# Splitting the second weights of the first token group, and letting the planner choose between GpSimd and VectorE for low parts

## Chip, cores and metric

One core of one Trainium2 chip runs the whole program as a single launch. The metric is the device time of that launch in microseconds (us). Engines are named as the profile names them: PE is TensorE (PEld its weight loads), DVE is VectorE, ACT is ScalarE, POOL is GpSimd, SP is SyncE, which here issues every DMA.

## What is computed

Top-32 attention over 2 batches x 8 heads x 576 rows, then a mixture of 4 experts over the 1152 tokens, then a gated block. Cut from the reference:

```python
scores = scale * np.matmul(q, k.transpose(0, 1, 3, 2))      # 576 x 576 per head
kth = np.partition(scores, -top_k, axis=-1)[..., -top_k:-top_k + 1]
scores = np.where(scores >= kth, scores, -1000000000.0)     # then softmax, then @ v
...
for e in range(E):                                          # E = 4, D = 512, F = 1024
    h = np.maximum(x @ w1[e], 0.0)
    out += p[:, e:e + 1] * (h @ w2[e])
...
a = x @ w_a
b = x @ w_b
return (a * b @ w_out).astype(np.float32)                   # d_ff = 1536
```

Everything is float32.

## The kernel before, in words

**Tokens and groups.** The 1152 tokens are nine tiles of 128. They go through attention and experts in four groups of 1, 2, 3 and 3 tiles (numbered 0 to 3). Attention of a tile takes four steps, one for each pair of heads: scores on PE, evicted by ACT (L702); four MAX8 and three MATCH_REPLACE8 for each of two heads on DVE (L722, L730) to find the 32nd largest score; mask and softmax on ACT and POOL (L753, L757, L761, L772); transposes on PE (L460), and the product with V. After the last step of a head pair, ACT and DVE write a group's attention output as a high and a low part into `xs` (L865, L867). While attention of a later group goes on, PE fills in the expert work of an earlier one.

**Two ways to multiply.** PE multiplies full float32 operands in one long matmul, which the trace shows as two records each. Or an operand is split into a high part (rounded to `fp32r`) and the low rest, and three short fp32r matmuls, high x high, high x low and low x high, take the place of one long one. `w_unit` splits a 512 KB piece of weights: load into `raw`, ACT writes the high part into `mid` (L888), and GpSimd or VectorE subtracts to make the low part (L889). In `experts`, which serves groups 1 to 3, all operands are split. Which of the two engines makes the low part is fixed in the code by `late`: GpSimd for group 1 and for experts 0 and 1 of group 2, VectorE for the rest.

**Group 0** has one tile, and `plain` serves it without splitting. Each expert takes two halves of 512 hidden units: 16 long matmuls of 128 columns with w1 into one PSUM bank `p`, one ACT Relu into `hf` (L1063), then 4 long matmuls of 512 columns with w2, which the trace names `ps<-raw,low` and `ps<-ys,low`. That is 32 of these for the group.

**What sets the order.** All work is recorded as operations with an engine, a length, a priority and dependencies. A planner (`Plan.best`, `order`) plays them through with a list of lengths, makes 42 orders with random delays, and emits the one whose replay is shortest on average. Each engine then runs its own list strictly in order, held back by semaphores alone. An operation that is late therefore holds everything behind it on its engine, and a change of one operation can move any other.

Of the kernel before, what the change touches and what calls it, by code (L numbers as in the profile page):

```python
# [79 lines left out]


class Op:
    __slots__ = ("engine", "hold", "lag", "key", "emit", "waits", "after", "tiles", "n", "start", "left", "at", "nbytes", "port", "since", "late")

# [11 lines left out]
class Plan:  # L96
# [3 lines left out]
    def add(self, engine, hold, emit, key, after=(), tiles=(), lag=100, nbytes=0, port=False):  # L100
        op = Op()
        op.engine, op.hold, op.lag, op.key, op.emit = engine, hold, lag, key, emit
        op.waits = list({id(a): a for a in after if a is not None}.values())
        op.tiles = list({id(t): t for t in tiles}.values())
        op.after, op.n, op.start, op.nbytes, op.port, op.since = [], len(self.ops), None, nbytes, port, 0.0
        op.late = 0.0
        self.ops.append(op)
        return op

    def best(self):  # L110

        found = None
        for r in range(ORDERS):
            draw = random.Random(r)

            since = STAGES[r * len(STAGES) // ORDERS]
            for op in self.ops:
                if r:  # L120
                    op.late = found[3][op.n] if found[4][op.n] < since else draw.uniform(0.0, SHAKE)
            got = self.order()
            mean = sum(self.rerun(got, random.Random(i)) for i in range(RERUNS)) / RERUNS
            if LOG:
                print("order", r, since, self.span, mean)
            if found is None or mean < found[0]:
                found = mean, got, {id(t): t.slot for op in got for t in op.tiles}, [op.late for op in self.ops], [op.start for op in self.ops]
        for op in found[1]:
            for t in op.tiles:
                t.slot = found[2][id(t)]  # L130
        return found[1]
# [30 lines left out]
    def order(self):  # L162
# [7 lines left out]
                t.users += 1  # L170
        for op in self.ops:
            op.left, op.at = len(op.waits), op.since
            for w in op.waits:
                w.after.append(op)
        late, ready, free, events, tick = {}, {}, {}, [], 0
# [42 lines left out]
        def pick(engine):  # L218
            late_, ready_ = late[engine], ready[engine]
            while late_ and late_[0][0] <= now:  # L220
                _, _, op = heapq.heappop(late_)
                heapq.heappush(ready_, (op.key, op.n, op))
            skipped, found = [], None
            stuck = set()
            while ready_:
                item = heapq.heappop(ready_)
                op = item[2]

                ok = not (op.port and free.get("POOL", 0.0) > now)
# [12 lines left out]
            return found  # L242

        while len(done) < len(self.ops):
            moved = False
            for engine in free:
# [8 lines left out]
                for t in op.tiles:  # L255
                    if t.slot is None:
                        t.slot = place(t)
                        t.slots.free.discard(t.slot)
                        t.slots.next += 1
                op.start = now  # L260
                done.append(op)
                if engine == "SP":
                    free[engine] = now + ISSUE
# [13 lines left out]
            while queue and queue[0][0] <= now:  # L277
# [10 lines left out]
                for a in op.after:  # L288
                    a.left -= 1
                    a.at = max(a.at, now + (SEEN_PE if a.engine == "PE" else SEEN))  # L290
                    if not a.left:
                        heapq.heappush(late[a.engine], (a.at, a.n, a))
# [10 lines left out]
def dve(n):  # L303
    return 62 + 1.04 * n


def pool_(n):
    return 105 + 2.2 * n
# [11 lines left out]
LATE = 2  # L320

FILL = 9
SLACK = 1200

URGENT = 3


def body(tc, q, k, v, probs, w1, w2, wa, wb, wo, out):
# [553 lines left out]
    def w_unit(src, a, late):  # L882
# [4 lines left out]
        ld = load(lambda: r.ap.rearrange("p (a n) -> p a n", a=a), lambda: src, 500 + s, (), [r], 512 << 10)  # L887
        hi = scalar(1024, lambda: nc.scalar.activation(u.ap[:, 0:1024], r.ap, AF.Copy), 500 + s, [ld], [u, r], sbuf=True)  # L888
        sub = lambda eng: eng.tensor_tensor(u.ap[:, 1024:2048], r.ap, u.ap[:, 0:1024], op=ALU.subtract)  # L889
        if late:  # L890
            lo = vector(dve(1024), lambda: sub(nc.vector), 500 + s if late > 1 else -100, [hi], [u, r], port=True)
        else:
            lo = gpsimd(pool_(1024), lambda: sub(nc.gpsimd), -100, [hi], [u, r])
        return u, [hi, lo], lambda i: u.ap[:, i * 1024:(i + 1) * 1024].rearrange("p (a n) -> p a n", a=a)

    plains = [0]
# [41 lines left out]
    def experts(c):  # L938
# [7 lines left out]
        yd, sums_ = {}, {}  # L946
        for e in range(E):

            late = 2 if c == len(GROUPS) - 1 else c == len(GROUPS) - 2 and e >= LATE
            for f0 in range(0, F, 512):  # L950
                hts, units = [], []
                for u in range(f0, f0 + 512, 256):
# [73 lines left out]
    def plain(c):  # L1026
# [5 lines left out]
        for e in range(E):  # L1032
            last2 = None
            for f0 in range(0, F, 512):
                p = ms.tile()
                p2 = p2 if f0 else ms.tile()
                h = hfs.tile()
                last = None
                us = []
                for u in range(0, 512, 256):  # L1040
# [11 lines left out]
                if e == 0 and f0 == 0:  # L1052

                    for a in range(KD):
# [5 lines left out]
                                )  # L1060

                        last = tensor(4 * mm_f(128), emit, 1000 + nxt(), [last] + us[0][1] + us[1][1] + xdone[c, a], [p, us[0][0], us[1][0]])
                hd = scalar(512, lambda h=h, p=p: nc.scalar.activation(h.ap, p.ap, AF.Relu), -1000, [last], [h, p])  # L1063
                for u in range(0, 512, 256):
                    r, rd, rv = plain_unit(w2[e, f0 + u:f0 + u + 256].rearrange("(a p) n -> p a n", p=128), 2)
# [166 lines left out]
```

## Time and profile before

| | |
|---|---|
| median of 3 runs | 841.64 us (841.16 to 842.02) |
| profiled execution, its device time | 841.12 us |
| its span, first to last instruction | 839.3 us |
| PE, DVE, ACT, POOL busy | 817.1, 707.0, 536.5, 266.0 us |
| mean granted TensorE clock | 0.997 |

The span is the profiled execution alone, and 1.8 us of its device time lie outside it. "Busy" is the union of an engine's instruction records. Records of one engine overlap a little, so the time that an instruction takes from its successor is read from start to start, not from its length.

### The profile page before, as it was taken

The numbers are of one execution on the slowest core, as the hardware profiler recorded it, in microseconds if no ns is written. First come the engines' busy times: TensorE is split into PE (matmuls) and PEld (weight loads), VectorE is DVE, ScalarE is ACT, GpSimd is POOL, SyncE is SP. The second block draws the span as 40 slices with busy tenths as digits, with TensorE's granted clock in tenths as the row PEclk, the third lists the DMA queues.
The fourth block names the chain that finished last, engine by engine and source line by source line (L and its number), as shares of the span: only waits on it lengthen the run. The fifth ranks groups of instructions, "written<-read, shape, count | busy, mean of one in ns | idle before, by whom it ended". The sixth has DMA issues, their size and how long they took to land.

```text
span 839.3 us, 14126 instructions
## 1 busy us (share of the span) xinstructions
PE 817.1 (97%) x5177; PEld 729.6 (87%) x5177; DVE 707.0 (84%) x1371; ACT 536.5 (64%) x1029; POOL 266.0 (32%) x250
## 2 busy tenths in 40 slices
PE   7599999999999999999999999999999999999997
PEld 6477787789888889889889998998898989999996
DVE  7999999999999999999969999545235889899723
ACT  6888887989989898887666555343125535344220
POOL 3634443897997966654110000000000000000000
PEclk9999999999999999999999999999999999999999
DMA  5849977755554445323345656443002322323003
GB/s 174 288 123 310 311 237 240 227 164 179 180 178 150 155 147 182 102 76 101 101 126 163 213 158 220 126 125 101 1 1 60 91 78 74 101 77 100 26 1 112
DMA packets 83509, 117.06 MB, mean 139 GB/s; under 512 B 10608, under 2 KB 54640, under 8 KB 83440
## 3 DMA queue, kind: packets, MB, share of 16 engines
q1 hardware_dynamic: 83440, 116.17, 44.0%
q8 instruction: 40, 0.66, 0.3%
q14 instruction: 29, 0.24, 0.1%
HBM read 109.07 MB, written 7.08 MB: 138 GB/s over the span
## 4 chain that ended last, share of the span: by engine, by line
PE 80%; DVE 16%; ACT 3%; issue 1%; POOL 0%; DVEq 0%; POOLq 0%; ACTq 0%
PE ps L457 75%; DVE low L722 8%; DVE low L730 7%; PE ps L460 4%; ACT low L772 1%; ACT mid L888 0%; POOL mid L889 0%; ACT low L827 0%; ACT low L702 0%; ACT low L753 0%; DVE low L793 0%; ACT low L761 0%; DVE low L1171 0%; DVE ys L1079 0%; DVE xs L867 0%
## 5 line engine op out<-in xcount | busy, mean ns | idle before, releaser
L722 DVE MAX8 low<-low 128x8 f32<-128x576 f32 x288 | 203.9, 747 | 1.7 <-ACT low L702 1.7
L457 PE MATMUL ps<-xs,mid 128*128 128x384 f32 (+1 forms) x1152 | 203.9, 321 | 0.0
L457 PE MATMUL ps<-mid 128*128 128x512 f32 x768 | 197.5, 395 | 0.4 <-POOL mid L889 0.4
L457 PEld LDWEIGHTS ps<-xs,mid 128*128 128x128 f32 x1152 | 185.1, 189 | 9.2 <-issue 1.9
L457 PEld LDWEIGHTS ps<-mid 128*128 128x128 f32 x768 | 139.6, 188 | 23.7 <-POOL mid L889 1.0
L730 DVE MATCH_REPLACE8 low<-low 128x576 f32<-128x576 f32 x216 | 159.4, 744 | 0.0
L457 PE MATMUL ps<-xs,big 128*128 128x384 f32 x864 | 152.6, 335 | 0.0
L457 PEld LDWEIGHTS ps<-xs,big 128*128 128x128 f32 x864 | 150.2, 188 | 1.5 <-DVE xs L1020 0.3
L888 ACT ACTIVATE mid<-raw 128x1024 fp32r<-128x1024 f32 x96 | 101.7, 1059 | 42.0 <-PE ps L457 31.8
L889 POOL TENSOR_TENSOR mid<-raw,mid 128x1024 fp32r<-128x1024 f32 x48 | 115.3, 2408 | 12.9 <-ACT mid L888 8.8
L757 POOL TENSOR_TENSOR low<-low 128x576 f32<-128x576 f32 x70 | 99.5, 1438 | 24.7 <-ACT low L753 24.3
L889 DVE TENSOR_TENSOR mid<-raw,mid 128x1024 fp32r<-128x1024 f32 x48 | 59.4, 1237 | 23.5 <-ACT mid L888 23.0
L958 ACT ACTIVATE mid<-ps 128x384 fp32r<-128x384 f32 (+1 forms) x96 | 43.4, 454 | 52.2 <-PE ps L457 51.5
L457 PE MATMUL ps<-big,mid 128*128 128x512 f32 x324 | 76.1, 391 | 0.0
L457 PEld LDWEIGHTS ps<-big,mid 128*128 128x128 f32 x324 | 60.5, 188 | 12.6 <-DVE low L1171 0.6
L962 DVE SCALAR_TENSOR_TENSOR mid<-ps,mid 128x384 fp32r<-128x384 f32 (+1 forms) x96 | 48.0, 506 | 23.0 <-ACT mid L958 22.8
L1150 ACT ACTIVATE low<-ps 128x384 f32<-128x384 f32 x36 | 17.7, 492 | 70.1 <-PE ps L457 70.0
L772 ACT ACTIVATE low<-low 128x576 f32<-128x576 f32 x70 | 51.1, 773 | 13.1 <-DVE low L769 13.1
L753 ACT ACTIVATE low<-low 128x576 f32<-128x576 f32 x70 | 52.2, 776 | 6.7 <-POOL low L747 6.7
L761 ACT ACTIVATE low<-low 128x576 f32<-128x576 f32 x70 | 54.3, 778 | 2.1 <-POOL low L757 1.8
L460 PE MATMUL ps<-identr,low 128*128 128x128 f32 (+1 forms) x360 | 51.1, 284 | 4.4 <-ACT low L772 3.8
L702 ACT ACTIVATE low<-ps 128x576 f32<-128x576 f32 x72 | 46.4, 649 | 11.9 <-POOL low L757 6.6
(90 smaller groups left out, 1025.9 us busy)
## 6 DMA issues: line engine op xcount, KB each, us to landing
raw<-in_moe_w_dram SPq DMA_DIRECT2D x122, 512.0 KB, 3.7
big<-kscr SPq DMA_DIRECT2D x20, 576.0 KB, 5.1
low<-in_v_dram SPq DMA_DIRECT2D x24, 256.0 KB, 3.6
low<-in_moe_w_a_dram SPq DMA_DIRECT2D x12, 512.0 KB, 4.2
low<-in_moe_w_b_dram SPq DMA_DIRECT2D x12, 512.0 KB, 3.8
low<-in_moe_w_out_dram SPq DMA_DIRECT2D x12, 512.0 KB, 3.6
kscr<-big SPq DMA_DIRECT2D x8, 576.0 KB, 4.7
ys<-in_moe_w_dram SPq DMA_DIRECT2D x6, 512.0 KB, 4.9
```

The costliest lines, as they stand in the source:

```text
L457: nc.tensor.matmul(out, l, r, **kw)
L460: nc.tensor.transpose(out, a, i)
L702: S, lambda: nc.scalar.activation(s.ap.rearrange("p (c n) -> p c n", c=2), at.ap[:, :, 0:HALF], AF.Copy),
L722: 62 + 1.04 * width, lambda at=at, cs=cs: nc.vector.max(m8v()[:, x, cs], at()), key + 0.02 * r, [done],
L730: lambda at=at, cs=cs: nc.vector.match_replace(out=src[1](), in_to_replace=m8v()[:, x, cs], in_values=at(), imm_value=LOW),
L753: S, lambda x=x, s=s: nc.scalar.activation(e[x].ap, s.ap, AF.Relu, bias=endv()[:, x, 1:2], scale=-STEEP),
L757: pool_(S), lambda x=x, s=s: nc.gpsimd.tensor_tensor(e[x].ap, s.ap, e[x].ap, op=ALU.subtract), ks, [a], [s, e[x]]
L761: lambda x=x: nc.scalar.activation(e[x].ap, e[x].ap, AF.Exp, bias=endv()[:, x, 0:1], scale=scale, accum_out=sums.ap[:, x:x + 1]),
L772: S, lambda x=x: nc.scalar.activation(e[x].ap, e[x].ap, AF.Copy, scale=sums.ap[:, x:x + 1]),
L888: hi = scalar(1024, lambda: nc.scalar.activation(u.ap[:, 0:1024], r.ap, AF.Copy), 500 + s, [ld], [u, r], sbuf=True)
L889: sub = lambda eng: eng.tensor_tensor(u.ap[:, 1024:2048], r.ap, u.ap[:, 0:1024], op=ALU.subtract)
L962: lambda h=h, p=p: nc.vector.scalar_tensor_tensor(h.ap[:, n:2 * n], p.ap[:, 0:n], 0.0, h.ap[:, 0:n], op0=ALU.max, op1=ALU.subtract),
```

## The change

`plain` takes the second weights of experts 1 to 3 of group 0 through `w_unit`. Relu now gives two tiles in `mid`: the high part by ACT and the low part by DVE, a SCALAR_TENSOR_TENSOR from PSUM. Each long matmul with w2 becomes three short ones. Expert 0 of the group keeps its eight long ones. Low parts made by `w_unit` get a second engine: the planner takes DVE where it is free first and POOL otherwise. Only experts 1 to 3 of group 3 keep DVE as a fixed choice. The core of the diff:

```diff
+                if op.start is not None:
+                    continue
+
+                ok = not ((op.port or engine != op.own[0]) and free.get("POOL", 0.0) > now)
...
+                if engine != op.own[0]:
+                    op.engine, op.hold, op.lag, op.key = op.other
+                    op.port = True
...
+                        for w in [a.engine] + ([a.other[0]] if a.other else []):
+                            heapq.heappush(late[w], (a.at, a.n, a))
...
+APART = (1, 2, 3)
...
-        if late:
-            lo = vector(dve(1024), lambda: sub(nc.vector), 500 + s if late > 1 else -100, [hi], [u, r], port=True)
+        if late > 2:
+            lo = vector(dve(1024), lambda: sub(nc.vector), 500 + s, [hi], [u, r], port=True)
         else:
-            lo = gpsimd(pool_(1024), lambda: sub(nc.gpsimd), -100, [hi], [u, r])
+            lo = gpsimd(pool_(1024), lambda: sub(nc.vector if lo.engine == "DVE" else nc.gpsimd), -100, [hi], [u, r])
+            if True:
+
+                lo.other = "DVE", dve(1024), 90, 490
...
-            late = 2 if c == len(GROUPS) - 1 else c == len(GROUPS) - 2 and e >= LATE
+            late = (2 if e == 0 else 3) if c == len(GROUPS) - 1 else c == len(GROUPS) - 2 and e >= LATE
...
+                if e in APART:
+
+                    hi, lo = hs_.tile(), hs_.tile()
+                    hd = [scalar(512, lambda h=hi, p=p: nc.scalar.activation(h.ap[:, 0:512], p.ap, AF.Relu), -1000, [last], [hi, p])]
+                    hd.append(vector(
+                        dve(512),
+                        lambda h=hi, l=lo, p=p: nc.vector.scalar_tensor_tensor(
+                            l.ap[:, 0:512], p.ap, 0.0, h.ap[:, 0:512], op0=ALU.max, op1=ALU.subtract
+                        ),
+                        -1000, hd, [hi, lo, p],
+                    ))
+                    for u in range(0, 512, 256):
+                        r, rd, rv = w_unit(w2[e, f0 + u:f0 + u + 256].rearrange("(a p) n -> p a n", p=128), 2, False)
+                        for i in range(2):
...
+                                for m, (a, w) in enumerate(((hi, 0), (hi, 1), (lo, 0))):
+                                    mm(p2.ap, a.ap[:, cs], rv(w)[:, i], start=(f == 0 and m == 0), stop=(f + 128 == F and m == 2))
+
+                            last2 = tensor(3 * mm_r(512), emit, 1000 + nxt(), [last2] + hd + rd, [p2, r, hi, lo])
+                    continue
```

Counted over the whole built program, the instructions that differ in number are these: PE 24 long matmuls of 512 columns fewer and 72 short ones more; ACT 12 high parts of weights more (its six Relu only change their target); DVE 6 low parts of hidden units more and 24 low parts of weights fewer (24 in place of 48); POOL 36 low parts of weights more (84 in place of 48). The number and size of the loads stay as they are, but the two w2 loads that went to `ys` now go to `raw`.

The change also moves other work, since the planner makes a new order. On DVE, the place is the end of group 0's experts, where DVE hands the attention output of group 1 to PE. First the list before (`xs<-ps,xs 128x256` is the low part of group 1's last head pair, MAX and MATCH_REPLACE are the top-k of group 2):

```order
L730 MATCH_REPLACE low<-low 128x576 x2
L722 MAX low<-low 128x8 x4
L730 MATCH_REPLACE low<-low 128x576 x2
L722 MAX low<-low 128x8
L867 TENSOR_TENSOR xs<-ps,xs 128x256
L722 MAX low<-low 128x8
```

And the list of the changed kernel at that place (`mid<-ps,mid 128x512` is the last of the six low parts of hidden units, `ys<-ps,pr,ys` adds an expert's output):

```order
L734 MAX low<-low 128x8 x4
L781 RECIPROCAL low<-low 128x2
L742 MATCH_REPLACE low<-low 128x576
L1083 SCALAR_TENSOR_TENSOR mid<-ps,mid 128x512
L742 MATCH_REPLACE low<-low 128x576
L734 MAX low<-low 128x8 x2
L742 MATCH_REPLACE low<-low 128x576 x2
L734 MAX low<-low 128x8 x2
L742 MATCH_REPLACE low<-low 128x576 x2
L734 MAX low<-low 128x8
L781 RECIPROCAL low<-low 128x2
L734 MAX low<-low 128x8
L1117 SCALAR_TENSOR_TENSOR ys<-ps,pr,ys 128x512
L879 TENSOR_TENSOR xs<-ps,xs 128x256
```

The `xs` part stands behind 107 MAX in the first list and behind 112 in the second, and six low parts of hidden units have come in ahead of it.

On PE, the same place: the last matmuls of group 0 (w2 of expert 3) and the first of group 1's experts (`xs,mid`). Before (`ps<-raw,low 128x512` is a long matmul with w2, `identr,low` are transposes of probabilities):

```order
L457 MATMUL ps<-xf,ys 128x128 x4
L460 MATMUL ps<-identr,big 128x128 x6
L457 MATMUL ps<-raw,low 128x512 x2
L457 MATMUL ps<-xs,mid 128x256 x3
L457 MATMUL ps<-raw,low 128x512
L457 MATMUL ps<-xs,mid 128x256 x3
L457 MATMUL ps<-raw,low 128x512
L457 MATMUL ps<-xs,mid 128x256 x6
L460 MATMUL ps<-identr,low 128x128 x4
```

In the changed kernel (`ps<-mid 128x512 x3` is one long matmul with w2 as three short ones):

```order
L469 MATMUL ps<-xf,ys 128x128 x8
L469 MATMUL ps<-mid 128x512 x3
L472 MATMUL ps<-identr,low 128x128 x4
L472 MATMUL ps<-identr,low 64x128
L472 MATMUL ps<-identr,low 128x128 x4
L472 MATMUL ps<-identr,low 64x128
L469 MATMUL ps<-mid 128x512 x3
L469 MATMUL ps<-xs,mid 128x256 x3
L469 MATMUL ps<-mid 128x512 x3
L469 MATMUL ps<-big 128x288 x4
L469 MATMUL ps<-low 64x128 x8
L469 MATMUL ps<-low,vrem_72 64x128 x2
```

The first matmuls with w2 now stand directly behind the w1 matmuls (`xf,ys`) whose Relu they need, and a whole step of attention (`identr,low` to `low,vrem`) stands between them and the rest of the first expert matmuls.

On POOL, low parts of weights now begin in the middle of group 1's attention (`low<-low 128x576` is the subtraction of the mask, `mid<-raw,mid` a low part of weights); before, the next 20 rows of the list have none:

```order
L769 TENSOR_TENSOR low<-low 128x576 x2
L901 TENSOR_TENSOR mid<-raw,mid 128x1024
L778 TENSOR_SCALAR low<-low 128x2
L901 TENSOR_TENSOR mid<-raw,mid 128x1024
L759 TENSOR_TENSOR low<-low,facs 128x4
L769 TENSOR_TENSOR low<-low 128x576 x2
L901 TENSOR_TENSOR mid<-raw,mid 128x1024
L778 TENSOR_SCALAR low<-low 128x2
```

All the 12 new low parts, and all the others that had the choice, stand in POOL's list.

## Rows read from the trace of the kernel before

**Rows 1.** The page: span, busy time of each engine, chain that ended last.

```profile
span 839.3 us, 14126 instructions
...
PE 817.1 (97%) x5177; PEld 729.6 (87%) x5177; DVE 707.0 (84%) x1371; ACT 536.5 (64%) x1029; POOL 266.0 (32%) x250
...
PE 80%; DVE 16%; ACT 3%; issue 1%; POOL 0%; DVEq 0%; POOLq 0%; ACTq 0%
```

**Rows 2.** Busy time by stretch: stretch, length, busy us and instructions of each engine.

```profile
60.00:160.00 100.00, 98.95 (x740) 77.59 (x741) 100.00 (x215) 85.78 (x175) 48.93 (x54) 1.00 0.85 269
160.00:440.00 280.00, 279.48 (x2092) 250.22 (x2092) 270.61 (x559) 240.66 (x481) 192.09 (x153) 1.00 0.45 144
```

**Rows 3.** Timeline of PE: start, us, instruction; pace of long and short w2 matmuls.

```profile
62.23 1.02 PE L457 MATMUL ps<-raw,low 128*128 128x512 f32 x2
63.09 1.05 PE L457 MATMUL ps<-xf,ys 128*128 128x128 f32 x8
...
451.81 4.72 PE L457 MATMUL ps<-mid 128*128 128x512 f32 x20
456.37 0.69 PE L457 MATMUL ps<-xs,mid 128*128 128x384 f32 x3
```

**Rows 4.** Groups of instructions: count | busy us, mean ns | idle before them.

```profile
L889 POOL TENSOR_TENSOR mid<-raw,mid 128x1024 fp32r<-128x1024 f32 x48 | 115.3, 2408 | 12.9 <-ACT mid L888 8.8 <-DVE low L722 2.0 <-DVE low L730 0.7
L888 ACT ACTIVATE mid<-raw 128x1024 fp32r<-128x1024 f32 x96 | 101.7, 1059 | 42.0 <-PE ps L457 31.8 <-issue 9.6 <-ACT low L1116 0.4
L889 DVE TENSOR_TENSOR mid<-raw,mid 128x1024 fp32r<-128x1024 f32 x48 | 59.4, 1237 | 23.5 <-ACT mid L888 23.0 <-PE ps L457 0.4
```

**Rows 5.** Timeline of DVE around the hand-over to group 1.

```profile
143.62 0.07 DVE L730 MATCH_VALUE_LOAD low<-low 128x8 f32 x1
...
144.34 0.08 DVE L730 MATCH_VALUE_LOAD low<-low 128x8 f32 x1
...
145.73 0.41 DVE L867 TENSOR_TENSOR xs<-ps,xs 128x256 fp32r<-128x256 f32 x1
146.05 0.75 DVE L722 MAX8 low<-low 128x8 f32<-128x576 f32 x1
...
154.37 0.75 DVE L1079 SCALAR_TENSOR_TENSOR ys<-ps,pr,ys 128x512 f32<-128x512 f32 x1
155.03 0.09 DVE L730 MATCH_VALUE_LOAD low<-low 128x8 f32 x1
```

**Rows 6.** Timeline of PE at the same place.

```profile
143.71 1.09 PE L457 MATMUL ps<-low 128*64 128x128 f32 x16
...
144.95 0.80 PE L457 MATMUL ps<-big 128*128 128x288 f32 x4
145.59 1.05 PE L457 MATMUL ps<-xf,ys 128*128 128x128 f32 x8
146.39 0.71 PE L460 MATMUL ps<-identr,big 128*128 128x128 f32 x6
146.94 1.13 PE L457 MATMUL ps<-xf,ys 128*128 128x128 f32 x8
...
153.94 1.43 PE L460 MATMUL ps<-identr,low 128*128 128x128 f32 x10
155.13 0.95 PE L457 MATMUL ps<-xs,mid 128*128 128x256 f32 x6
...
158.85 3.76 PE L457 MATMUL ps<-xs,mid 128*128 128x256 f32 x30
162.45 2.62 PE L457 MATMUL ps<-mid 128*128 128x512 f32 x10
```

**Rows 7.** Busy time from the first new split to the end of attention for group 1.

```profile
77.00:140.00 63.00, 62.85 (x479) 49.45 (x478) 63.00 (x138) 53.63 (x112) 26.08 (x32) 1.00 0.86 282
```

**Rows 8.** Waits of PE from 160 to 440 us: releaser: us, times, longest.

```profile
PE ps L457 <- POOL mid L889: 0.4, 1, 0.4
```

**Rows 9.** The stretch in which the granted clock falls (third last column).

```profile
39.00:47.00 8.00, 6.27 (x45) 5.24 (x46) 8.00 (x18) 7.81 (x19) 4.84 (x8) 0.79 0.10 18
```

More of the change, by code (lines that the diff above doesn't have):

```diff
@@ L82 @@
 class Op:
-    __slots__ = ("engine", "hold", "lag", "key", "emit", "waits", "after", "tiles", "n", "start", "left", "at", "nbytes", "port", "since", "late")
+    __slots__ = ("engine", "hold", "lag", "key", "emit", "waits", "after", "tiles", "n", "start", "left", "at", "nbytes", "port", "late", "since", "other", "own")
 SEEN, SEEN_PE = 45, 130
@@ L106, in add @@
         op.late = 0.0
+        op.other, op.own = None, (engine, hold, lag, key, port)
         self.ops.append(op)
@@ L126, in best @@
             if found is None or mean < found[0]:
-                found = mean, got, {id(t): t.slot for op in got for t in op.tiles}, [op.late for op in self.ops], [op.start for op in self.ops]
+                found = mean, got, {id(t): t.slot for op in got for t in op.tiles}, [op.late for op in self.ops], [op.start for op in self.ops], [op.engine for op in self.ops]
         for op in found[1]:
+            op.engine = found[5][op.n]
             for t in op.tiles:
@@ L172, in order @@
             op.left, op.at = len(op.waits), op.since
+            op.engine, op.hold, op.lag, op.key, op.port = op.own
             for w in op.waits:
@@ L221, in pick @@
                 _, _, op = heapq.heappop(late_)
-                heapq.heappush(ready_, (op.key, op.n, op))
+                heapq.heappush(ready_, (op.key if engine == op.own[0] else op.other[3], op.n, op))
             skipped, found = [], None
@@ L227, in pick @@
                 op = item[2]
-                ok = not (op.port and free.get("POOL", 0.0) > now)
+                if op.start is not None:
+                    continue
+                ok = not ((op.port or engine != op.own[0]) and free.get("POOL", 0.0) > now)
                 for t in op.tiles:
@@ L291, in order @@
                     if not a.left:
-                        heapq.heappush(late[a.engine], (a.at, a.n, a))
+                        for w in [a.engine] + ([a.other[0]] if a.other else []):
+                            heapq.heappush(late[w], (a.at, a.n, a))
                         heapq.heappush(queue, (a.at, -1, None))
@@ L1036, in plain @@
                 p2 = p2 if f0 else ms.tile()
-                h = hfs.tile()
                 last = None
@@ L1062, in plain, with emit @@
                         last = tensor(4 * mm_f(128), emit, 1000 + nxt(), [last] + us[0][1] + us[1][1] + xdone[c, a], [p, us[0][0], us[1][0]])
+                if e in APART:
[11 more added lines that the diff above has]
+                        for i in range(2):
+                            f = f0 + u + i * 128
+                            def emit(f=f, s=u // 128 + i, i=i, rv=rv, hi=hi, lo=lo, p2=p2):
+                                cs = slice(s * 128, (s + 1) * 128)
+                                for m, (a, w) in enumerate(((hi, 0), (hi, 1), (lo, 0))):
+                                    mm(p2.ap, a.ap[:, cs], rv(w)[:, i], start=(f == 0 and m == 0), stop=(f + 128 == F and m == 2))
+                            last2 = tensor(3 * mm_r(512), emit, 1000 + nxt(), [last2] + hd + rd, [p2, r, hi, lo])
+                    continue
+                h = hfs.tile()
                 hd = scalar(512, lambda h=h, p=p: nc.scalar.activation(h.ap, p.ap, AF.Relu), -1000, [last], [h, p])
```

## The prediction

> **What bounds the kernel now.** I read the page first. PE is busy for 817.1 of 839.3 us, and the chain of work that ended last runs over PE for 80% and over DVE for 16% [rows 1]. This looks like a kernel in which whatever is taken off PE comes off the time. The next view is busy time by stretch, because the change acts in one stretch: the first long w2 matmul of those shown runs at 62 us [rows 3], and group 0's experts end where group 1's begin, near 155 us. From 60 to 160 us PE is busy for 98.95 of 100 us, but DVE is busy for 100.00 of 100 us [rows 2]. The reader is to see that two engines are full at once. Work taken off one of them is worth nothing where the other's list holds it back. ACT has 14 us free there and POOL 51. From 160 to 440 us PE is busy for 279.48 of 280 us [rows 2], and its waits there add up to 0.4 us [rows 8]. So from the first experts of group 1 on, PE alone sets the end: the end moves by as much as that start moves, plus what PE gains or loses behind it.
>
> So the question is when PE gets to group 1's experts. I take one place that both lists have, and behind which both hold the same work: the second of six matmuls `xs,mid` that stand behind the w2 matmuls of group 0. In the list as built it is the first that waits for DVE's `xs` part of the last head pair. Behind it the changed list holds the same PE instructions as before, but for five transposes of probabilities more and four transposes of `ys` fewer (0.1 us). Before, PE runs it at 155.25 us: the six begin at 155.13, and one takes 0.12, from 30 in the 3.60 us between 158.85 and 162.45 [rows 6].
>
> **The change part by part.**
>
> *PE, less work.* A long w2 matmul takes 0.86 us from its start to the next one's (62.23 to 63.09), a short one 0.228 us (20 of them from 451.81 to 456.37) [rows 3]. 24 x 0.86 = 20.6 us go and 72 x 0.228 = 16.4 us come: 4.2 us less. By PE's work alone the place would be reached at 155.25 - 4.2 = 151.0 us.
>
> *DVE, more work in the full stretch.* Each half of an expert now needs a low part of 512 hidden units, a SCALAR_TENSOR_TENSOR from PSUM, which the trace does not show in this size. The nearest rows are the accumulation of 512 columns from PSUM, 0.66 us to the next start (154.37 to 155.03), and twice a subtraction of 256 columns from PSUM, 2 x 0.32 = 0.64 us (145.73 to 146.05) [rows 5]. I take 0.65, so six make 3.9 us. A gain is excluded: nothing leaves DVE's list ahead of this place. I counted both lists. Up to the sixth of these low parts, the changed list holds exactly what the list of before holds up to its 79th MATCH_REPLACE (106 MAX and all else equal), plus the six. That MATCH_REPLACE begins at 143.62 and gives way to the next at 144.34 [rows 5]. DVE has no pause there [rows 2], so the sixth low part cannot end before 144.34 + 3.9 = 148.2 us.
>
> *PE, held by it.* The third short matmul of expert 3's second half multiplies this low part. PE's list then holds, up to the place: 10 short w2 matmuls (2.3 us), 13 expert matmuls (13 x 0.12 = 1.6), 15 transposes of probabilities (10 in 155.13 - 153.94 = 1.19, so 1.8), 12 of queries (six in 146.94 - 146.39 = 0.55, so 1.1), two lots of four score matmuls (145.59 - 144.95 = 0.64 each, 1.3), one product with V (144.95 - 143.71 = 1.24) and 4 transposes of `ys` (0.5, as those of probabilities) [rows 6]. That is 9.8 us, so the place comes at 158.0 us, 2.7 us later than before. The saved 4.2 us are all used up, and about 7 us (158.0 - 151.0) of new waiting shows on PE ahead of the place. The bounds: some of these prices hold a switch between kinds of matmuls, and at 0.5 us less in all the shift is 2.2 us; below that it cannot go as long as DVE's rows cost what they did.
>
> *ACT, more work.* Twelve high parts at 1.06 us [rows 4] are 12.7 us. From 77 to 140 us ACT was busy for 53.63 of 63 us [rows 7]; over the 71 us from 77 to 148 that rate makes 60.4 us. With the twelve it is 73.1 us, 2.1 us more than there is. Records overlap a little, so the true excess lies between nothing and 2.1 us. ACT feeds both the low parts and the top-k, so what it lacks delays DVE. I take 0.7 us, nearer to nothing, since the changed list still lets DVE go on with top-k meanwhile.
>
> *POOL.* Twelve low parts at 2.41 us [rows 4] are 28.9 us in a stretch with 51 us free; hidden. Without that cover each would hold a mask subtraction for up to 2.4 us, and a softmax behind it. The 24 low parts that go from DVE to POOL are 24 x 1.24 = 29.8 us less on DVE [rows 4], but all in groups 2 and 3, where PE hardly waits: 0.4 us at most to gain [rows 8]. POOL has 88 us free from 160 to 440 us [rows 2] and nothing to do after. The w2 loads are as many as before; two go to another buffer. Nothing is queued behind them that PE waited for in the trace.
>
> *Sum.* 2.7 + 0.1 + 0.7 = 3.5 us. The profiled execution took 841.12 us, so 844.6; the median of the runs is 841.64, 0.52 more, so I predict 845.1 us.
>
> **A price from the clock.** PE's new idle time, 7 us in pieces over some 75 us, has a risk of its own. From 39 to 47 us, where PE was busy for only 6.27 of 8 us, the granted clock averaged 0.79 [rows 9], so part of it ran at 1.2 GHz and the rest at 2.4: 8 x 0.21 = 1.7 us of PE work were lost. The Trainium skill, in TensorE: Matmul & The Clock Gate, section HAM oscillation, warns that idle gaps send the clock back to half rate and that each such fall costs its warm-up again. By this rule the change pays for its gaps, which is the third rival below; by the full-clock rows alone it pays nothing.
>
> **The rivals.**
>
> *The saved matmul time comes off the end.* 841.64 - 4.2 = 837.4 us. For it speak PE's share of the chain and its 98.95 of 100 us. It needs DVE not to hold PE, so the six low parts to end by 141 us, 7 us before DVE's list can give the last one. I see no row that shortens that list. Chance 0.10, mostly for an error in my counting.
>
> *Nearly nothing changes.* The shift at the hand-over is 2.2 us, ACT's excess is nothing, and PE wins back its 0.4 us of waiting and a little of the switching between the two kinds of matmuls, which falls away for the 24: 841.64 + 2.2 - 0.4 - 0.5 = 842.9, and less if more falls away. Chance 0.20.
>
> *The clock falls.* If it falls once in the last 10 us ahead of the place or behind it, 1.7 us come on top: 846.8 us; twice, 848.5. A fall earlier than 148 us costs nothing, because PE waits for DVE there anyway. It is decided by whether PE's new gaps lie together or apart. Against it: PE still has some 90% to do. Chance 0.12.
>
> *The likeliest*, a hand-over delayed by DVE's list with PE at full clock: 843.4 to 847.0 us, around 845.1. Chance 0.58.
>
> **How the numbers follow.** About 0.2% (1.7 us) is what a measurement of this kernel tells from no change, so "same" is 840.0 to 843.3 us. Faster is the first rival, 0.10. Same is the second, 0.20. Slower is the third and the likeliest, 0.70. The range leaves out the first rival and the far end of the third, where the clock falls twice: 840.5 to 848.5 us.
>
> **What would show it.** In the profile after: PE busy for some 92 of 100 us from 60 to 160 us, DVE still at 100. PE's largest new waits in that stretch end with the low parts of hidden units (L1083) or with the Relu ahead of them (L1080). The last L1083 ends at 148 us or later. The `xs` part L879 of the last head pair follows it, and the second of six `xs,mid` matmuls comes near 158 us. ACT is at 95% or more from 77 to 148 us. POOL's 12 low parts are at 2.4 us each, and DVE is idle for longer from 400 us on, without a change of the end. The prediction is wrong if the last L1083 ends before 144 us; if L1083 takes much less than 0.6 us; or if PE, once in group 1, makes up time that the trace of before does not show as waiting.

## The result, and the profile after

The changed kernel takes 847.38 us (median of four runs, 847.23 to 847.61) against 841.4 us for the kernel before (four runs, 841.12 to 842.02): a ratio of 1.0071, 95% interval 1.0058 to 1.0083. It is slower, as predicted, and inside the range, but by 6.0 us and not by 3.5, and above the 847.0 us up to which the likeliest case went. Its profiled execution took 847.46 us, 6.34 more than the one of before.

The first view is the page after: span, busy time, and the chain that ended last.

```profile
span 845.7 us, 14212 instructions
...
PE 814.0 (96%) x5201; PEld 735.2 (87%) x5201; DVE 700.4 (83%) x1353; ACT 546.7 (65%) x1041; POOL 353.0 (42%) x286
...
PE 81%; DVE 7%; ACT 6%; POOL 2%; DMA 2%; issue 2%; POOLq 0%; ACTq 0%
```

Against [rows 1], PE is busy for 3.1 us less and the span is 6.4 us longer. DVE's share of the chain fell from 16% to 7%; ACT, POOL and a DMA came in. Next, busy time by stretch (start and end, length, then PE, PEld, DVE, ACT, POOL, granted clock, DMA share, GB/s):

```profile
0.00:60.00 60.00, 42.51 (x268) 36.21 (x270) 51.85 (x117) 44.30 (x96) 24.78 (x43) 0.72 0.58 176
60.00:160.00 100.00, 92.03 (x729) 77.97 (x726) 99.97 (x214) 91.07 (x176) 73.41 (x62) 1.00 0.82 266
160.00:440.00 280.00, 279.38 (x2102) 252.73 (x2103) 264.71 (x563) 246.72 (x495) 217.90 (x168) 1.00 0.45 144
39.00:47.00 8.00, 4.96 (x23) 4.21 (x23) 8.00 (x18) 5.71 (x13) 4.64 (x7) 0.60 0.23 50
47.00:51.00 4.00, 4.00 (x28) 3.39 (x28) 3.26 (x10) 3.05 (x8) 1.68 (x3) 0.51 0.01 3
```

From 60 to 160 us PE is busy for 92.03 of 100 us, where [rows 2] had 98.95; DVE is as full as before. Behind 160 us PE works as it did. In the start the clock stands lower than in [rows 9], and down to 51 us: 0.51 from 47 to 51 us, where before it was back at 1.00. (The 0.72 of the first row can't be set against the kernel before: its trace records no clock ahead of 34.8 us, where its matmuls ran at the half pace too, from 15 to 25 us the 288-column ones at 0.24 us each, against 0.135 at full clock.) Now PE's waits in the stretch ahead of group 1 (us, times, longest):

```profile
PE ps L472 <- ACT low L784: 3.7, 3, 2.3
PE ps L472 <- ACT low L714: 1.1, 1, 1.1
PE ps L469 <- DVE mid L1083: 0.9, 1, 0.9
PE ps L469 <- DMA raw<-in_moe_w_dram: 0.9, 1, 0.9
PE ps L469 <- ACT mid L1080: 0.7, 1, 0.7
PE ps L469 <- ACT low L1101: 0.5, 1, 0.5
```

They add up to 7.8 us from 60 to 165 us. The largest are not the ones that the prediction looked for, L1083 or L1080 (0.9 and 0.7 us), but L784, the scaled softmax weights. And 0.9 us went to a load, where the prediction saw none that PE would wait for. And DVE's waits from 0 to 60 us:

```profile
DVE low L781 <- POOL low L778: 2.3, 3, 1.3
DVE big L527 <- ACT big L525: 2.0, 2, 1.8
DVE identr L493 <- POOL xf masks.py:199: 1.3, 1, 1.3
DVE low L805 <- ACT low L799: 1.2, 1, 1.2
DVE low L734 <- ACT low L714: 0.9, 1, 0.9
```

The same view of before has none at the RECIPROCAL, which is L781 here and was L769:

```profile
DVE big L515 <- ACT big L513: 1.8, 2, 1.7
DVE low L722 <- ACT low L702: 1.4, 1, 1.4
DVE identr L481 <- POOL xf masks.py:199: 1.3, 1, 1.3
```

That is 4.5 us before and 7.7 after. The timeline shows the rows (start, duration, what; in brackets the idle time before it):

```profile
27.14 0.17 DVE L781 RECIPROCAL low<-low 128x2 f32<-128x2 f32 x1 [0.54 <-POOL low L778]
36.85 0.17 DVE L781 RECIPROCAL low<-low 128x2 f32<-128x2 f32 x1 [1.28 <-POOL low L778]
47.85 0.17 DVE L781 RECIPROCAL low<-low 128x2 f32<-128x2 f32 x1 [0.47 <-POOL low L778]
52.02 0.82 DVE L805 SCALAR_TENSOR_TENSOR low<-low 128x576 f32<-128x576 f32 x1 [1.19 <-ACT low L799]
...
112.82 2.38 POOL L901 TENSOR_TENSOR mid<-raw,mid 128x1024 fp32r<-128x1024 f32 x1 [1.14 <-ACT mid L900]
113.41 0.75 DVE L1117 SCALAR_TENSOR_TENSOR ys<-ps,pr,ys 128x512 f32<-128x512 f32 x1
115.09 0.59 ACT L1080 ACTIVATE mid<-ps 128x512 fp32r<-128x512 f32 x1
115.28 0.21 POOL L778 TENSOR_SCALAR low<-low 128x2 f32<-128x2 f32 x1
115.53 0.16 DVE L781 RECIPROCAL low<-low 128x2 f32<-128x2 f32 x1
115.73 1.44 ACT L784 ACTIVATE low<-low 128x576 f32<-128x576 f32 x2
116.56 0.76 PE L472 MATMUL ps<-identr,low 128*128 128x128 f32 x5 [2.29 <-ACT low L784]
...
151.04 0.68 DVE L1083 SCALAR_TENSOR_TENSOR mid<-ps,mid 128x512 fp32r<-128x512 f32 x1
161.43 0.96 PE L469 MATMUL ps<-xs,mid 128*128 128x256 f32 x6
```

Above, DVE's new pauses: 0.54 + 1.28 + 0.47 + 1.19 = 3.5 us. In the new order these rows stand ahead of MAX rows that they used to follow, and DVE stands still for the softmax chain (exp on ACT, sum on POOL). Below, the place of the prediction: the second of the six `xs,mid` of the last row runs at 161.6 us by its own record. Before, the six began at 155.13 [rows 6], here at 161.43: 6.3 us later, the whole of what the execution lost. The middle rows are taken up below.

To compare kernels of different content I count PE's work: each matmul at the median distance from its shape's start to the next start behind 60 us, over all runs. "Done" is that sum at 60 us; "left" is the rest at 180 us, when group 0's experts are over. The last column is the profiled execution against before's 841.12; the runs are from several chips, on which the medians of the kernel before differ by up to 0.7 us.

```
kernel               done at 60   left at 180   against before   execution
before                  27.8         638.6             -              -
after                   25.6         645.1           +6.5           +6.3
after, e8               27.1         642.0           +3.4           +3.4
before, e9              26.1         640.5           +2.0           +2.0
after, e10              25.3         640.9           +2.3           +5.4
before, e11             24.6         644.4           +5.9           +5.2
```

By this count the change took 4.1 us of work off PE (776.4 to 772.3), as predicted. At 60 us PE is 2.2 us behind; from 60 to 180 us it does 101.6 in place of 110.0 us, of which 4.1 no longer exist and 4.3 were lost. So two losses are to be explained: 2.2 us in the start, and in the stretch behind it 4.3 us on top of the whole saving.

### The profile page after: what moved, and what is told of

It is laid out like the page before. It is cut to its first block, busy times and chain, and to the rows that moved or that the text cites. A ratio compares the mean times of both kernels' runs of the same rounds, so it can differ in the third digit from the quotient of the medians.

```text
span 845.7 us, 14212 instructions
## 1 busy us (share of the span) xinstructions
PE 814.0 (96%) x5201; PEld 735.2 (87%) x5201; DVE 700.4 (83%) x1353; ACT 546.7 (65%) x1041; POOL 353.0 (42%) x286
## 4 chain that ended last, share of the span: by engine, by line
PE 81%; DVE 7%; ACT 6%; POOL 2%; DMA 2%; issue 2%; POOLq 0%; ACTq 0%
PE ps L469 75%; PE ps L472 6%; DVE low L734 2%; DVE low L742 2%; POOL big L529 1%; DMA low<-in_q_dram 1%; ACT low L784 1%; ACT low L773 1%; POOL low L769 1%; ACT low L765 1%; ACT low L839 1%; ACT low L714 1%; POOL mid L901 0%; ACT mid L900 0%; DMA low<-in_moe_w_a_dram 0%
## 5 line engine op out<-in xcount | busy, mean ns | idle before, releaser
L901 POOL TENSOR_TENSOR mid<-raw,mid 128x1024 fp32r<-128x1024 f32 x84 | 204.2, 2434 | 47.0 <-ACT mid L900 41.5
L469 PE MATMUL ps<-mid 128*128 128x512 f32 x840 | 219.1, 396 | 2.5 <-DVE mid L1083 0.9
L469 PEld LDWEIGHTS ps<-mid 128*128 128x128 f32 x840 | 151.3, 188 | 28.4 <-DVE mid L1083 1.7
L900 ACT ACTIVATE mid<-raw 128x1024 fp32r<-128x1024 f32 x108 | 114.0, 1058 | 35.3 <-PE ps L469 32.4
L769 POOL TENSOR_TENSOR low<-low 128x576 f32<-128x576 f32 x70 | 99.0, 1432 | 23.5 <-ACT low L765 22.5
L714 ACT ACTIVATE low<-ps 128x576 f32<-128x576 f32 x72 | 46.7, 650 | 13.3 <-POOL low L769 10.5
L784 ACT ACTIVATE low<-low 128x576 f32<-128x576 f32 x70 | 51.5, 780 | 5.7 <-DVE low L781 5.7
L469 PE MATMUL ps<-big 128*128 128x288 f32 x256 | 52.3, 332 | 0.8 <-ACT low L714 0.8
```

What stands on the lines that cost most here:

```text
L469: nc.tensor.matmul(out, l, r, **kw)
L714: S, lambda: nc.scalar.activation(s.ap.rearrange("p (c n) -> p c n", c=2), at.ap[:, :, 0:HALF], AF.Copy),
L769: pool_(S), lambda x=x, s=s: nc.gpsimd.tensor_tensor(e[x].ap, s.ap, e[x].ap, op=ALU.subtract), ks, [a], [s, e[x]]
L784: S, lambda x=x: nc.scalar.activation(e[x].ap, e[x].ap, AF.Copy, scale=sums.ap[:, x:x + 1]),
```

## The experiments

Each run is compared with the kernel before on the same chip. In the expectations, "group 1's experts" and "group 1's second to fourth expert" mean the first group's, which the text above calls group 0. The function `later` of some runs moves rows of VectorE's list by so many places and merges the lists again so that all dependencies hold; the lists of the other engines stay as they were.

**e1: the RECIPROCALs later.**

```diff
+    moves = list(zip(early, (1, 2, 1))) + [(hurry[1], 1), (hurry[0], 1)]
...
-    for op in plan.best():
+    for op in later(plan.best()):
```

> The changed kernel with one edit: in VectorE's list the RECIPROCALs of the first three steps stand one, two and one rows later, and the first L805 stands behind one MAX of the next step; every other list is the same. My theory: VectorE's list sets when group 1's last head pair ends, and the changed kernel's list pauses 0.54, 1.28, 0.47 and 1.19 us at these four rows, 3.5 us in all, which the list before did not. Without the pauses the place moves 3.5 us ahead and the time goes from 847.4 to 843.9 us, 845 if half of the first scores come late then. Rival one, only the six added SCALAR_TENSOR_TENSORs and the weights' splits cost: 847.4, no change, since VectorE would wait elsewhere. Rival two, the clock that falls to half around 41 to 51 us costs it: 847.4 with the same fall of the clock.

848.45 us, ratio 1.0076 (1.0063 to 1.0088): no gain. The pauses at these four rows went from 3.5 to 0.2 us, but others of DVE grew, so that its waits up to 60 us fell by 2.1 us (7.7 to 5.6), and PE runs its row of 151.77 us at 150.43, 1.3 us earlier and not 3.5:

```profile
DVE low L781 <- POOL low L778: 0.2, 1, 0.2
150.43 0.50 PE L469 MATMUL ps<-mid 128*128 128x512 f32 x1 [1.03 <-DVE mid L1083]
```

Then the clock takes that back (windows, columns as above):

```profile
148.00:151.00 3.00, 1.30 (x6) 0.83 (x7) 3.00 (x8) 2.44 (x4) 2.83 (x4) 1.00 0.64 208
151.00:155.00 4.00, 4.00 (x18) 3.44 (x17) 4.00 (x9) 4.00 (x10) 4.00 (x4) 0.57 0.69 230
```

Behind a stretch with 1.30 of 3 us busy, PE ran at a mean of 0.57 for 4 us: 1.7 us of work lost. The profiled execution is the fastest of the five (847.21 us); whether the clock fell in the others too isn't known. So this run doesn't decide on the pauses, but it doesn't bear out their full price either.

**e2: the added VectorE rows short.**

```diff
-l.ap[:, 0:512], p.ap, 0.0, h.ap[:, 0:512], op0=ALU.max, op1=ALU.subtract
+l.ap[:, 0:16], p.ap[:, 0:16], 0.0, h.ap[:, 0:16], op0=ALU.max, op1=ALU.subtract
```

> The changed kernel with the same lists, but the six SCALAR_TENSOR_TENSORs (L1083) work on 16 of 512 columns, and the third matmul takes the high part of the hidden values in place of the low part, so that the low part of the hidden values is left out. My theory: VectorE's list holds the end of the stage, so six rows of about 0.1 us in place of 0.69 us give back 6 x 0.57 = 3.4 us: 844.0 us. Rival, TensorE or ScalarE holds it: 847.4 us, no change.

847.7 us, 1.0067 (1.0054 to 1.0081): nothing, as the rival said. The six rows took 163 ns each in place of 683, and yet PE's longest wait for L784 stands at the same place, no earlier and no shorter than the 2.29 us at 116.56 above:

```profile
117.28 0.76 PE L472 MATMUL ps<-identr,low 128*128 128x128 f32 x5 [2.36 <-ACT low L784]
```

This is where my theory fell: VectorE's six added rows are not, by themselves, what the end waits for.

**e3: both edits.** Diffs as in e1 and e2.

> Both edits: the later RECIPROCALs and the six short SCALAR_TENSOR_TENSORs, lists else the same; the low part of the hidden values is left out. My theory: the two add up, 3.5 + 3.4 = 6.9 us, which is less than the 7.8 us that TensorE waits between 60 and 165 us in the changed kernel: 840.5 us, near the kernel before without being much under it, since TensorE's saving of 4.2 us would then begin to show; 842 if ScalarE (66.1 of 71 us busy between 77 and 148 us) holds TensorE before that. Rival, TensorE's clock or order sets the time: over 845 us.

846.93 us, 1.006 (1.0048 to 1.0073), far from 840.5. The rival, over 845, holds for the number. Its clock fell at 151 us as in e1.

**e4: the free choice of engine alone.**

```diff
-APART = (1, 2, 3)
+APART = ()
```

> The changed kernel with no expert's second weights taken apart: only the choice between GpSimd and VectorE for the low parts, and the order that follows from it, are left of the change. VectorE's rows of the first stage come out the same as in the changed kernel, with the RECIPROCALs of the first steps ahead of the rows that they followed before. My theory: its place is late by the pauses of the start alone, 3.5 us, and has no added SCALAR_TENSOR_TENSORs: about 841.4 + 3.5 = 844.9 us. Rival, the pauses cost nothing and only taking the weights apart does: 841.4 us.

845.96 us, 1.0051 (1.0039 to 1.0064), nearer to the theory than to the rival. PE's work was 2.1 us behind at 60 us and no more than 2.0 at 180. The rest, some 2.8 us, was lost later, most of it in a fall of the clock:

```profile
460.00:468.00 8.00, 6.17 (x27) 5.84 (x26) 5.93 (x8) 3.43 (x6) 3.73 (x2) 0.79 0.68 197
```

So the theory came near in the number by some luck: the start cost 2 us and not 3.5. What the run does show is the stretch from 60 to 180 us: with DVE's pauses in the start, but without the weights taken apart, PE did 110.2 us of work there, as before (110.0), and is busy for 98.71 of the 100 us from 60 to 160. In the changed kernel that stretch holds the larger loss. It comes in with the taking apart, or with the order that the planner then makes.

**e5, e6: the taking apart of the weights short, on POOL alone and on POOL and ACT.**

```diff
-sub = lambda eng: eng.tensor_tensor(u.ap[:, 1024:2048], r.ap, u.ap[:, 0:1024], op=ALU.subtract)
+sub = lambda eng: eng.tensor_tensor(u.ap[:, 1024:1024 + m], r.ap[:, 0:m], u.ap[:, 0:m], op=ALU.subtract)
...
-r, rd, rv = w_unit(w2[...], 2, False)
+r, rd, rv = w_unit(w2[...], 2, False, 16)
... in e6 also
-hi = scalar(1024, lambda: nc.scalar.activation(u.ap[:, 0:1024], r.ap, AF.Copy), ...
+hi = scalar(1024, lambda: nc.scalar.activation(u.ap[:, 0:m], r.ap[:, 0:m], AF.Copy), ...
```

> The changed kernel with the same lists; of the second weights of group 1's second to fourth expert GpSimd takes only 16 of 1024 columns of each unit's low part (L901, 12 units), and the matmul with the low weights takes the high ones, so that these low parts are left out. The first theory has fallen with the shortened SCALAR_TENSOR_TENSORs, which gave nothing; the new one is that the taking apart of the weights stands inside the softmax chain in the in-order lists: TensorE waits 3.7 us for the scaled weights (L784), ahead of which stand L901 on GpSimd (2.4 us each, ahead of L778) and L900 on ScalarE (1.05 us each). If GpSimd's part is what holds the chain, the time falls by most of 3.7 us, to about 844 us. Rival, ScalarE's part holds it: it falls by the one wait that L901 sets alone, about 0.9 us at 116 us, to 846.5 us. Rival two, neither: 847.4 us.

> As the run before, and ScalarE too takes only 16 of 1024 columns of these 12 units (L900); the matmuls take the hidden values as their right side, so the second weights are left out. Lists as in the changed kernel. New theory (the taking apart stands in the softmax chain on ScalarE and GpSimd): the waits of TensorE for L784 (3.7 us), for L714 (1.1) and for L1080 (0.7) go for the most part, so 4 to 5 us: 842.5 to 843.5 us, and the VectorE row L1083 shows 0.9 us of wait or is covered. Rival, the order of the lists and the start hold the time: 847.4 us.

e5: 846.99 us, 1.0067 (1.0053 to 1.0081), the second rival or, within the interval, the first. The theory, 844, missed. e6: 849.21 us, 1.009 (1.0072 to 1.0108), with runs from 847.24 to 852.37: with less to do on ACT and POOL the kernel was not faster, and its median was slower. The theory, 843.5 at most, missed, and the rival's 847.4 is at the lower end of the runs. Its profiled execution, the slowest of them, shows why that one was: three falls of the clock, each worth 6 x 0.28 = 1.7 us:

```profile
104.00:110.00 6.00, 5.05 (x26) 4.72 (x27) 6.00 (x13) 3.12 (x7) 3.75 (x5) 0.72 0.95 327
118.00:124.00 6.00, 4.96 (x24) 4.08 (x26) 6.00 (x13) 4.33 (x10) 1.62 (x2) 0.72 0.77 261
155.00:161.00 6.00, 5.31 (x24) 4.64 (x24) 6.00 (x14) 5.21 (x12) 5.92 (x5) 0.72 0.30 98
```

**e7, e8: with the later RECIPROCALs, and then with the short VectorE rows too.** Diffs as in e1, e2 and e6.

> As the run before, with the RECIPROCALs of the first three steps and the first L805 later in VectorE's list. Alone, that made the stage up to 150 us 1.4 us shorter, and a fall of the granted clock to half at 151 us, behind the waits of 148 to 151 us, took it back. Without those waits the clock should stand, and the 1.4 us should show: 841 to 842 us. Rival, the start costs nothing at the end: the time of the run before.

> As the run before, and the six SCALAR_TENSOR_TENSORs (L1083) on 16 of 512 columns: nearly all that the change adds to ScalarE, GpSimd and VectorE is gone (second weights and the low part of the hidden values are left out), and TensorE's shorter list is left. If added work on the three engines and the start are the whole loss, TensorE's 4.2 us come out: 841.4 - 4.2 + 0.9 (what the start still lags by at 60 us) = 838.1 us. Rival, VectorE's list still holds the stage (it is 0.9 us later than before by the start, and has no added work): 841 to 842 us, and TensorE waits for it.

e7: 847.46 us, 1.0072 (1.005 to 1.0095). The theory missed. The six runs fall into three from 845.1 to 845.8 and three from 849.1 to 851.3 us, so the median is a time that none of them took, and whether the rival, e6's time, holds can't be told. The profiled one, of the faster three, has a fall of the clock at 150 us again. e8: 845.95 us, 1.0045 (1.0033 to 1.0057), where the theory said 838.1 and the rival 842 at most, so both missed. With nearly all added work gone, PE's list shorter by 4.1 us, and the start 0.7 us behind, this list order is still slower than the kernel before by 0.45%, and PE still waits 7.3 us from 60 to 165 us. Each taken against the kernel before on its chip, the changed kernel loses 6.0 us and e8 3.9, so in this order the added work and the start's rows together are worth some 2 us. What is left must lie in the order of the lists, or in what is left of the added rows. What holds PE in e8 is seen in its timeline:

```profile
111.61 0.75 DVE L1117 SCALAR_TENSOR_TENSOR ys<-ps,pr,ys 128x512 f32<-128x512 f32 x1 [0.53 <-PE ps L469]
113.74 0.15 DVE L781 RECIPROCAL low<-low 128x2 f32<-128x2 f32 x1
113.93 1.44 ACT L784 ACTIVATE low<-low 128x576 f32<-128x576 f32 x2 [0.83 <-DVE low L781]
114.75 0.77 PE L472 MATMUL ps<-identr,low 128*128 128x128 f32 x5 [2.29 <-ACT low L784]
```

It is a ring. DVE waits for PE's last w2 matmul of an expert (L1117), has two MATCH_REPLACE and then the RECIPROCAL behind it in its list, and PE's next instruction waits for that RECIPROCAL through ACT. A faster DVE only arrives earlier at its own wait. The same wait stands at this place in the other runs of this order:

```profile
115.27 0.77 PE L472 MATMUL ps<-identr,low 128*128 128x128 f32 x5 [2.29 <-ACT low L784]
116.15 0.77 PE L472 MATMUL ps<-identr,low 128*128 128x128 f32 x5 [2.29 <-ACT low L784]
119.04 1.31 PE L472 MATMUL ps<-identr,low 128*128 128x128 f32 x5 [2.29 <-ACT low L784]
```

These are e1, e5 and e6; e3, e7 and the changed kernel have 2.29 us too, e2 2.36. From the start of L1117 to that of PE's row it is 3.14 or 3.15 us in all of them but e2 (3.21). So the length of this wait hangs neither on the pauses of the start nor on what ACT, DVE and POOL have to do for the taking apart, but on the rows of the ring. Two shorter waits of PE, for L714 near 90 us (1.06 to 1.08 us) and for L1080 near 150 (0.69), also keep their length in all eight; with the ring they are 4.05 of the 7.8 us of the changed kernel, and the kernel before has none of the three. In the changed kernel (middle rows of its timeline above) DVE's RECIPROCAL stands at 115.53, POOL's L778 ends at 115.49 behind an L901, and ACT's L1080 ends at 115.68, all within 0.2 us: three lists are late together there as well. No run moved the rows of the ring in this order, so what it costs the end by itself is not shown.

**e9: the kernel before with its RECIPROCALs earlier.**

```diff
+    moves = list(zip(early, (-3, -4, -3)))
```

> The kernel before with one edit: the RECIPROCALs (L769) of the first three steps stand three, four and three rows earlier in VectorE's list, which makes its first rows the same as in the changed kernel; every other list is the same. In the kernel before VectorE has no wait from 52 us to the end of group 1, so a pause in the start should stand in the end. GpSimd's sums (L766) are there at 27.3, 37.3 and 46.2 us, the moved rows would come at 27.0, 35.3 and 45.7 us: pauses of 0.3, 2.0 and, counted from the list as then shifted, 0 us. First theory's price: 841.6 + 2.3 = 843.9 us. Rival, the pauses cost nothing, since TensorE or ScalarE are as late anyway: 841.6 us. Rival two, they also make the clock stay at half longer (3.4 us of it before, 10.3 us in the changed kernel), and TensorE is behind by more: 844.5 to 846 us.

843.9 us, 1.0027 (1.0016 to 1.0038): what the theory said, to a tenth, though by the runs on the same chip it is 2.6 us more than before and not the 2.3 looked for. Two of DVE's waits from 0 to 60 us, and the windows:

```profile
DVE low L769 <- POOL low L766: 1.6, 1, 1.6
...
DVE low L793 <- ACT low L787: 0.5, 1, 0.5
```

```profile
0.00:60.00 60.00, 43.39 (x274) 35.97 (x274) 53.25 (x120) 44.44 (x97) 24.63 (x43) 0.72 0.58 178
60.00:160.00 100.00, 98.86 (x746) 77.68 (x744) 100.00 (x217) 85.88 (x176) 47.72 (x54) 1.00 0.84 271
```

Three rows of 0.15 us, moved by three or four places, cost 0.27%. The stretch from 60 to 160 us is as full as before and only begins later. With the pauses the clock stood at half until 50.3 us instead of 45.0, so the run does not part what the pauses cost from what that costs PE.

**e10, e11: other draws in the search for an order**, for the changed kernel and for the one before.

```diff
-            draw = random.Random(r)
+            draw = random.Random(r + 4000)
```

> The changed kernel, with other draws in the search over 42 orders (the seeds 4000 to 4041 in place of 0 to 41): the same work in another order, in whose VectorE list the RECIPROCALs of the first steps stand behind the rows that they followed before. New theory: three engines reach the same places in group 1's experts at the same time (at 115.5 us VectorE's RECIPROCAL, GpSimd's L778 and ScalarE's L1080 end within 0.2 us), so that no part of the added work alone holds the time, and what the change costs hangs on the order that the search ends at: another order differs by some us, 843 to 849, and by the later RECIPROCALs rather 845. Rival, the added work sets the time whatever the order: 846.5 to 848 us.

> The kernel before, with other draws in its search (seeds 2000 to 2041): the same work in another order. It is the control for the run above: if orders alone move the time by some us, this one differs from 841.6 us by 1 to 4 us, to the slower side rather, since the order before was the better one of its search: 843 us. Rival, the order is worth little: 841 to 842.5 us.

e10: 846.41 us, 1.0054 (1.0042 to 1.0066). e11: 845.03 us, 1.0042 (1.003 to 1.0054). So the kernel before, the same work in another order of its own planner, is 3.8 us slower than itself: that is the theory of e11. The changed kernel with other draws is 1.4 us slower than that, but the intervals overlap, so this is not clear of the noise. e10 doesn't part its theory from its rival: 846.4 us lies in the theory's 843 to 849 and next to the rival's 846.5 to 848. In e10 PE's waits from 60 to 165 us are short:

```profile
PE ps L469 <- DVE mid L1083: 1.1, 2, 0.9
PE ps L469 <- ACT mid L1080: 0.7, 1, 0.7
PE ps L469 <- ACT low L1101: 0.5, 1, 0.5
```

There all the added work stands in the lists, and PE waits for 2.7 us and not for 7.8; of the three waits that kept their length, only the 0.69 us for L1080 is left. The time is lost in the start (2.5 us less done at 60 us) and behind 180 us (3.1 us), of which PE's waits there show 1.8; the rest stays open.

**e12: e10 with the start's rows later.**

```diff
+    moves = [(early[0], 1), (early[1], 3), (hurry[1], 3), (hurry[0], 1)]
```

> The order of the other draws for the changed kernel (846.4 us), with one edit: in VectorE's list the first two RECIPROCALs stand one and three rows later, and the two L805 one and three rows later; every other list is the same. That order's VectorE still pauses 0.3 and 1.8 us at these RECIPROCALs and 1.2 and 0.8 us at L805, but TensorE waits only 2.7 us between 60 and 165 us, against 7.8 us in the changed kernel. Theory: pauses in the start cost the end their full length where nothing else is as late, as in the kernel before (2.6 us for 2.3 us looked for): the rows that now fill the pauses give back 0.3 + 1.8 + 0.7 + 0.8 = 3.5 us, 843 us, 844 if half of one is left. Rival, the changed kernel's start isn't what costs, since there the same edit gave nothing: 846.4 us. The kernel before stays ahead in either case.

849.53 us, 1.0101 (1.0084 to 1.0118): slower by some 3 us, and neither theory nor rival. PE's waits in the start show a new one:

```profile
PE ps L472 <- DVE low L810: 2.1, 1, 2.1
```

L810 ends the hurried softmax of L805, which I had moved behind two MATCH_REPLACE; PE's transposes wait for it until 55.6 us, and behind that the clock stood at half once more, from 57.3 to 60.7 us. Then DVE, ahead for three steps (the third step's last MAX ends at 37.6 and not 40.6 us), stood still for 3.0 us ahead of a RECIPROCAL at 72.3 us. A pause filled at one place came back at another.

## Why the prediction was right or wrong

*PE's saving* was right: 4.2 us forecast, 4.1 counted. *That DVE's list is full and the gain is used up* was right in the numbers: DVE 99.97 of 100 us, PE 92.03 of 100 (92 forecast), waits of 7.8 us (7 forecast). That DVE's list is the reason was not, as e2 shows. *PE's list between the last low part and the place*: 9.9 us (151.7 to 161.6) against 9.8. *POOL hidden*: nothing clear of the noise came back in e5. *ACT's excess*, 0.7 us: DVE waited for ACT nowhere between 60 and 160 us, so nothing by that way, though PE's longest waits end with ACT's L784; ACT was busy for 66.1 of 71 us from 77 to 148 us, 93% and not the 95% forecast.

*The step that failed* is "DVE, more work in the full stretch". It took the time base of before, a MATCH_REPLACE at 143.62 us, for the changed list, and with it assumed that nothing changes ahead of 60 us. The last L1083 was to end at 148.2 us and ended at 151.72. The 3.5 us that it came later match the new pauses at the RECIPROCALs and at L805 in the first 52 us (3.5 us; 3.2 by all of DVE's waits up to 60 us). I had looked for pauses in the trace of before alone, in the full stretch; the lists showed the RECIPROCALs in other places, and I didn't price that. e9 shows the price in the kernel before: 2.3 to 2.6 us. Added to the forecast, it gives 847.4 to 847.7.

*That sum is not the cause, though.* It takes DVE's list as the one thing that PE waits for. e2 took 3.1 us (6 x 0.52) off that list and gained nothing; e5 took POOL's part, e8 nearly everything, and 0.45% stayed. Of PE's 7.8 us of waits, 4.05 kept their length in all these runs, and e10, with another order and all the added work, is without 3.4 of them. So what PE loses from 60 to 180 us goes with the order in which the planner's lists meet, and not with the amount of added work on one engine. That is argued from waits of the same length, not shown by a run that changes those rows alone. The sentence that a clock fall ahead of 148 us costs nothing was wrong as well: in e6 PE's work was 2.7 us behind the changed kernel's at 120 us and 4.7 at 180, behind falls at 105, 119 and 157 us of 1.7 us each. The rival of the falling clock had its mechanism in e1, e3, e6 and e7, but not in the changed kernel: there the clock was low for the last time from 40.7 to 50.9 us (before, from 41.6 to 45.0).

*Luck.* 847.4 us lies above the likeliest case and where the rival of the falling clock stood (846.8 for one fall, 848.5 for two). The range reached that far for falls near 148 us or later, which did not come; the time got there by another way. So the direction was foreseen, and that the time lies inside the range is in part luck.

*What stays open* is how much of the 6.0 us is the change and how much the order that was drawn. With two orders each, the changed kernel took 847.4 and 846.4 us, the one before 841.4 and 845.0: between 1.4 us, which is not clear of the noise, and 6.0 us. More draws would tell; no version tried here beats the kernel before.

## What to carry to other kernels

Where a planner makes the order, a change is two changes: read the new lists at every place where an engine's list was gapless before, the start too, and price each row that now stands ahead of what feeds it. Before work taken off one engine is counted as a gain, look at what the others do at the same place. And set the waits of several runs side by side: one that keeps its length to a hundredth of a us, whichever engine is relieved, may be a ring that starts at the waiting engine itself, and then it is the order of the rows that has to change. And run the kernel before in another order of its own: what it loses or gains there is a scale for how small a difference can be credited to an edit that also makes a new order.

## What the hardware showed that I had not expected

Which runs lost the clock did not go by the amount of work. In the changed kernel the clock stood through PE's 7.8 us of waits from 60 to 165 us. In the profiled execution of e1, with 8.2 us of them by the same view, it fell to the 1.2 GHz level once, at 151 us; so it did in e3 and e7, and three times in e6, with less work on the other engines. But in e2, e5 and e8, which have less work too, it stood. Each fall lasted 3.4 us and cost some 1.7 us of PE's work. Ahead of the one in e1, PE had waited for 0.69 and 1.03 us and was busy for 1.30 of 3 us; at the same place the changed kernel has 0.69 and 0.94 us, 1.37 of 3 us busy (149 to 152 us), and no fall. One execution of each kernel was profiled, so it stays open whether a fall goes with the kernel or with the execution. The Trainium skill, in TensorE: Matmul & The Clock Gate, section HAM oscillation, says that idle gaps bring the half rate back. The traces agree in that the falls of e1 and e7 stand behind gaps, but nearly equal gaps did and did not bring it.
